# Top-k attention with a routed MLP: the comparison of row tile 7 written with an accumulator output

## The chip, the cores and the metric

The kernel runs on one core of a Trainium2 chip. The metric is the device time of one execution in microseconds (us), and the number that counts is the median of several runs.

The engines are named as in the profile: PE is TensorE's matmul, PEld its weight load, DVE is VectorE, ACT is ScalarE, POOL is GpSimd, SP is SyncE, which issues most of the DMA transfers.

## The reference

Attention of 8 batches, 8 heads, 576 tokens, head size 64. Only the 32 highest scores of each row take part in the softmax. The result then goes through a layer that skips some tokens and sends each of the others to one of 8 experts.

```python
scores = scale * np.matmul(q, k.transpose(0, 1, 3, 2))
kth = np.partition(scores, -top_k, axis=-1)[..., -top_k:-top_k + 1]
mask = scores >= kth
scores = np.where(mask, scores, -1000000000.0)
...
attn = attn / (np.sum(attn, axis=-1, keepdims=True) + 1e-09)
return np.matmul(attn, v).astype(np.float32)

skip_score = x @ w_skip
do_compute = skip_score > 0
...
e_idx = np.argmax(logits, axis=1)
...
    h = np.maximum(xc[mask] @ w1[e], 0.0)
    y[mask] = gate_w[mask, None] * (h @ w2[e])
out[do_compute] = xc + y
```

## The kernel before

**Tiling.** The 64 heads are taken in 32 pairs. The two heads of a pair have 2 x 576 rows of scores, which are cut into nine row tiles of 128 rows, numbered `i` = 0 to 8; the middle one holds 64 rows of each head. A row tile of pair `p` has the running number `s = 9 p + i`.

**What is done for a row tile** (`row`, line 651):
- PE computes the 128 x 576 scores into one of three PSUM row buffers `r` (`qk`, line 670).
- DVE finds the eight highest of each of seven chunks (`chunk`, line 679, tile `cand`) and from these the 24 highest of the row (`cand`, lines 685 and 687, tile `cl`).
- ACT copies the scores out of PSUM into an SBUF tile `xc` (`take`, line 698); `xc` has three buffers. With this the PSUM row buffer is free again.
- ACT marks what is above the 24th score and counts it (`above_out`, line 693, with an accumulator output, which the profile shows as an instruction of its own on ACT).
- POOL multiplies the marked scores (`push_out`, line 701) and writes seven fill values (`fill`, line 710), both into `xw`.
- DVE takes the eight highest of `xw` (`window`, line 720, tile `wn`); the eighth is the 32nd highest score.
- The penalty is then written: a 128 x 576 tile in bf16 that is not zero where the score is below the 32nd highest (`below_out`, line 712, tile `PEN`). For seven of the nine row tiles it is an activation on ACT (line 717). For the two in `BELOW = (3, 7)` (line 28) it is a `tensor_scalar` on DVE (line 715).

**What uses it.** Per pair, PE computes the scores again, transposed, and adds the penalties with matmuls of `PEN` against `nbi`, which hold -2^120 on the diagonal (`block`, line 811). ACT exponentiates (line 832, `PT` and `PR`), and PE multiplies with the values (lines 879 to 898). POOL also adds two of the exponentials (line 858) and splits the next pair's inputs into high and low parts (lines 580 and 583).

**What sets the order.** The instructions of the attention part are put in order before the build by a planner (`Plan`, line 181): each task has an engine, an assumed duration and a due time from hand-set tables, and every engine then runs its list in that order. The planner's duration for the penalty on DVE is 0.42 us (line 748), in both kernels. A wait that matters below is in line 741: `take` of row tile `s` may start only when the penalty of row tile `s - 3` has been written (`OUTB[-3:-2]`), since both use the same buffer of `xc`. So the penalty of row tile 7 holds back `take` of row tile 1 of the next pair.

After the attention part (up to about 870 us) follow the experts (lines 1037 to 1223), which the change does not touch.

Of the kernel before, what the change touches and what calls it, by code (L numbers as in the profile page):

```python
# [9 lines left out]
F32 = mybir.dt.float32  # L10
# [4 lines left out]
OP = mybir.AluOpType  # L15
# [12 lines left out]
BELOW = (3, 7)  # L28
# [12 lines left out]
def tile_kernel(ctx, tc, q, k, v, w_skip, w_gate, w1, w2, out):  # L41
    nc = tc.nc
# [4 lines left out]
    P = 128  # L47
# [15 lines left out]
    cp = ctx.enter_context(tc.tile_pool(name="cp", bufs=1))  # L63
# [587 lines left out]
    def row(s):  # L651
        p, i = divmod(s, NR)
        i2 = p % NQ
        PEN[p] = PEN_[p % 2]
        h = Hold(RW, 1)
# [56 lines left out]
        def below_out():  # L712
            pen, least = PEN[p][:, PS * i + REM:PS * (i + 1)], WN[p][:, i, 7:8]
            if i in BELOW:
                nc.vector.tensor_scalar(pen, XC[s], least, None, op0=OP.is_lt)
            else:
                nc.scalar.activation(pen, XC[s], AF.Relu, bias=least, scale=-1.0)  # L717

# [27 lines left out]
        OUTW.append(wx)  # L746
        WINS.setdefault(p, []).append(wx)
        kx = PENNED[s] = A(*(("DVE", 0.42) if i in BELOW else ("ACT", 0.672)), s + D_["rf"] + J("rf"), below_out, wx, TU.get(p - 2))
        OUTB.append(kx)
        if i == NR - 1:  # L750
            FLAGGED[p] = A("POOL", 0.47, s + 3, flags, kx, WINS[p])

    XC, XW, OUTB, OUTW, WINS, PUSHD = {}, {}, [], [], {}, {}
    PS = S + REM
    PEN_ = [(ap_ if j == (NP - 1) % 2 else sp_).tile([P, NR * PS + REM], BF, name=f"PEN{j}") for j in range(2)]
    for t in PEN_:
        nc.vector.memset(t[:, 0:NR * PS].rearrange("p (i c) -> p i c", c=PS)[:, :, 0:REM], 0.0)
        nc.vector.memset(t[:, NR * PS:], 0.0)

# [32 lines left out]
    def block(p, whats, rb, turned):  # L792
# [5 lines left out]
        for half in range(2):  # L798
# [6 lines left out]
            for y, (h, c0, m, o, kc) in enumerate(whats):  # L805
                for c, i, a, z in hv[y][half][2]:
                    penalties.append((half, rb[:, O + c:O + c + z - a], PEN[p][:, PS * i + REM + c0 - o:PS * i + REM + c0 - o + P], nbi[:, a:z]))
        todo = penalties + products if turned else products + penalties
# [753 lines left out]
```

## Time and profile before

| what | value |
|---|---|
| time, median of 3 runs | 1147.55 us (1146.78, 1147.55, 1151.96) |
| time of the profiled execution | 1154.68 us |
| its span, from the first to the last instruction | 1152.8 us |
| PE busy | 1102.5 us, 96% of the span |
| DVE busy | 985.7 us, 85% |
| ACT busy | 889.3 us, 77% |
| POOL busy | 806.6 us, 70% |
| mean granted TensorE clock | 0.979 of full speed |
| DVE line 715, both row tiles, 64 instructions | 64.2 us busy, 1002 ns mean |

The busy shares are means over the whole span. In the attention part PE and DVE are both busy for some 98% of a pair's time, so which of them sets the time is read from the idle stretches of single pairs and from what ended them. The times of single instructions come from the profiled execution, which took 7.1 us longer than the median of the runs.

### The profile page before, as it was taken

Reading aid. Unit: us, or ns where it says so; the run is one execution under the profiler, and the core shown is the slowest. Engines: PE = TensorE matmul, PEld = TensorE weight load, DVE = VectorE, ACT = ScalarE, POOL = GpSimd, SP = SyncE. Lnnn points to the kernel's source line nnn. Section 1 sums busy time; section 2 is a strip of 40 time slices with the busy share of each in tenths; the row PEclk is TensorE's granted clock in tenths of the full one; section 3 lists DMA queues with packets and bytes.
Section 4 is the critical chain, followed back from the end, with each engine's and each line's share of the span. In section 5 each row is a group of like instructions: output and inputs, shape, how many; then the busy total and the mean of one; then the engine's idle time right before and its main releaser. Section 6 shows DMA issues by size and latency. Waiting matters only on the chain.

```text
span 1152.8 us, 37624 instructions
## 1 busy us (share of the span) xinstructions
PE 1102.5 (96%) x12995; PEld 934.2 (81%) x12995; DVE 985.7 (85%) x5002; ACT 889.3 (77%) x1838; POOL 806.6 (70%) x1236
## 2 busy tenths in 40 slices
PE   7799999999899999999998999999999999999996
PEld 5678888888788888888787888888787888999995
DVE  7999999999999999999999999999986556755541
ACT  4889999999799999998998999999884534444420
POOL 5878888888688888988998988888895212222211
PEclk7899999999899999999999999999999999999998
DMA  5655555665555555665654465555238465555300
GB/s 114 145 133 116 136 125 124 139 138 135 122 115 117 132 130 115 141 147 112 145 116 105 106 141 135 121 122 111 64 90 282 149 206 164 173 176 165 120 19 26
DMA packets 239257, 149.08 MB, mean 129 GB/s; under 512 B 141656, under 2 KB 204632, under 8 KB 239056
## 3 DMA queue, kind: packets, MB, share of 16 engines
q1 hardware_dynamic: 232192, 136.19, 48.5%
q0 software_dynamic: 3840, 9.47, 2.4%
q8 instruction: 105, 1.72, 0.6%
q10 hardware_dynamic: 3024, 0.90, 0.3%
q14 instruction: 96, 0.79, 0.2%
HBM read 76.57 MB, written 25.31 MB: 88 GB/s over the span
## 4 chain that ended last, share of the span: by engine, by line
PE 65%; DVE 19%; ACT 5%; issue 4%; SPq 2%; POOL 2%; DMA 1%; ACTq 0%; POOLq 0%; DVEq 0%
PE r L811 14%; PE r L670 11%; PE pa L879 7%; DVE cand L679 7%; PE py L1168 4%; PE py L1170 4%; PE py L1169 4%; PE ph L1145 3%; PE ph L1146 3%; PE ph L1147 3%; DVE wn L720 3%; DVE cl L685 3%; DVE cand L687 2%; PE pa L896 2%; PE pa L882 2%
## 5 line engine op out<-in xcount | busy, mean ns | idle before, releaser
L679 DVE MAX8 cand<-r 128x8 f32<-128x82 f32 (+1 forms) x2016 | 391.3, 233 | 11.2 <-PE r L670 7.2
L701 POOL TENSOR_TENSOR xw<-xc,r 128x576 f32<-128x576 f32 x288 | 370.6, 1287 | 19.2 <-ACT r L693 18.8
L693 ACT ACTIVATE r<-xc,cl 128x576 bf16<-128x576 f32 x288 | 226.5, 787 | 22.3 <-DVE cl L685 17.6
L720 DVE MAX8 wn<-xw 128x8 f32<-128x583 f32 x288 | 215.8, 750 | 3.3 <-POOL xw L701 3.3
L698 ACT ACTIVATE xc<-r 128x576 f32<-128x576 f32 x288 | 188.9, 657 | 32.0 <-DVE cl L685 24.0
L811 PE MATMUL r<-QH,KK 128*128 128x320 f32 (+1 forms) x640 | 184.1, 315 | 1.2 <-ACT xc L698 0.5
L670 PE MATMUL r<-KK,QH 128*128 128x288 f32 x640 | 159.0, 338 | 22.8 <-ACT xc L698 15.4
L717 ACT ACTIVATE PEN<-xc,wn 128x576 bf16<-128x576 f32 x224 | 176.2, 789 | 2.8 <-DVE wn L720 2.5
L811 PE MATMUL r<-QL,KK 66*128 66x320 f32 (+1 forms) x640 | 174.0, 299 | 0.0
L832 ACT ACTIVATE PT<-r 128x576 f32<-128x576 f32 x256 | 164.1, 652 | 7.9 <-PE r L811 7.5
L685 DVE MAX8 cl<-cand 128x8 f32<-128x28 f32 (+2 forms) x864 | 162.2, 188 | 2.3
L1074 POOL DMA_INDIRECT out_dram<-ot,idx x24 | 24.4, 1015 | 189.2 <-DVE ot L1073 144.8
L670 PEld LDWEIGHTS r<-KK,QH 128*128 128x128 f32 x640 | 97.8, 193 | 61.4 <-ACT xc L698 24.3
L670 PE MATMUL r<-KK,QL 65*128 65x288 f32 x640 | 135.1, 302 | 1.5 <-DMA QL<-LO 1.3
L1037 ACT ACTIVATE hi<-raw 128x1024 fp32r<-128x1024 f32 x64 | 67.2, 1056 | 78.6 <-PE py L1170 70.6
L811 PE MATMUL r<-nbi,PEN 128*128 128x128 bf16 (+1 forms) x1632 | 127.4, 216 | 0.3
L1040 DVE TENSOR_TENSOR lo<-raw,hi 128x1024 fp32r<-128x1024 f32 x60 | 73.2, 1223 | 61.7 <-ACT hi L1037 61.3
L879 PE MATMUL pa<-PT,V 128*32 128x256 f32 (+1 forms) x2464 | 122.5, 330 | 0.7 <-ACT os L905 0.4
L811 PEld LDWEIGHTS r<-QH,KK 128*128 128x128 f32 x640 | 118.7, 191 | 3.5 <-ACT xc L698 2.0
L811 PEld LDWEIGHTS r<-QL,KK 66*128 66x128 f32 x640 | 119.8, 193 | 0.0
L710 POOL TENSOR_TENSOR xw<-wo,CN 128x7 f32<-128x7 f32 x288 | 64.7, 225 | 73.6 <-ACT r L693 68.4
L811 PEld LDWEIGHTS <-PEN 128*128 128x128 bf16 x1632 | 88.6, 99 | 21.5 <-issue 3.1
(277 smaller groups left out, 2548.1 us busy)
## 6 DMA issues: line engine op xcount, KB each, us to landing
raw<-in_moe_w_dram SPq DMA_DIRECT2D x64, 512.0 KB, 3.5
KK<-HI SPq DMA_DIRECT2D x62, 288.0 KB, 4.2
QH<-HI SPq DMA_DIRECT2D x124, 144.0 KB, 4.1
KK<-LO SPq DMA_DIRECT2D x62, 144.0 KB
QL<-LO SPq DMA_DIRECT2D x62, 144.0 KB, 2.7
raw<-in_k_dram SPq DMA_DIRECT2D x64, 128.0 KB, 2.6
V<-in_v_dram SPq DMA_DIRECT2D x32, 256.0 KB, 3.2
out_dram<-xd SPq DMA_DIRECT2D x28, 288.0 KB, 3.3
```

The costliest lines, as they stand in the source:

```text
L670: nc.tensor.matmul(R(u, w), t[0:k0, c:c + P], KH[i2][0:k0, HB * hd + u:HB * hd + w], start=(k0 == P and x == 0), stop=(k0 < P and x == len ...
L679: nc.vector.max(C[s][:, c], R(CH[c], CH[c + 1]))
L685: nc.vector.max(L[:, 4 * r:4 * r + 8], c)
L693: nc.scalar.activation(RR[s], XC[s], AF.Sign, bias=CL[p][:, i, 23:24], scale=-ODD / SMALL, accum_out=CN[:, s:s + 1])
L698: nc.scalar.activation(XC[s], R(), AF.Copy, scale=SMALL)
L701: nc.gpsimd.tensor_tensor(xw()[:, 0:S], XC[s], RR[s], op=OP.mult)
L717: nc.scalar.activation(pen, XC[s], AF.Relu, bias=least, scale=-1.0)
L720: nc.vector.max(WN[p][:, i], XW[s])
L811: nc.tensor.matmul(*ops, start=half not in [x[0] for x in todo[:j]], stop=half not in rest, skip_group_check=turned)
L832: return pl.add("ACT", 0.535, due + K["ex"] + FINE["ex"][at], lambda: nc.scalar.activation(dst, st["r"], AF.Exp, scale=scale), x, give=[h])
L879: nc.tensor.matmul(o, vt[:, a, kc, w:w + 32], pts[a][:, kc, qs:qs + n], start=(kc == 0), stop=False, tile_position=(0, 64 * u + w))
L1040: eng.tensor_tensor(WLO[w][i], WRAW[w][i], WHI[w][i], op=OP.subtract)
```

## The change

The penalty of row tile 7 gets a second scalar operation (add 0.0), which leaves its values as they are, and an accumulator output into a new tile `under` of one value per row, which nothing reads. The penalty of row tile 3 stays as it was. The planner sees the same tasks with the same durations, and every engine has the same instructions in the same order with the same waits, but for the form of these 32 instructions.

```diff
@@ -712,7 +712,10 @@
         def below_out():
             pen, least = PEN[p][:, PS * i + REM:PS * (i + 1)], WN[p][:, i, 7:8]
             if i in BELOW:
-                nc.vector.tensor_scalar(pen, XC[s], least, None, op0=OP.is_lt)
+                if i == BELOW[0]:
+                    nc.vector.tensor_scalar(pen, XC[s], least, None, op0=OP.is_lt)
+                else:
+                    nc.vector.tensor_scalar(pen, XC[s], least, 0.0, op0=OP.is_lt, op1=OP.add, accum_out=under)
             else:
                 nc.scalar.activation(pen, XC[s], AF.Relu, bias=least, scale=-1.0)
 
@@ -752,6 +755,7 @@
 
     XC, XW, OUTB, OUTW, WINS, PUSHD = {}, {}, [], [], {}, {}
     PS = S + REM
+    under = cp.tile([P, 1], F32, name="under")
```

## Rows read from the trace of the kernel before

**Rows 1.** Two pairs: length, busy us (count) of PE, PEld, DVE, ACT, POOL, PEclk, DMA.
```profile
225.63:251.07 25.44, 24.98 (x356) 20.97 (x356) 25.23 (x147) 24.12 (x54) 21.76 (x34) 1.00 0.58 130
...
302.27:332.70 30.43, 27.16 (x354) 23.00 (x353) 27.83 (x147) 24.34 (x54) 21.10 (x34) 0.89 0.48 109
```
**Rows 2.** PE around 227 us, by time: start, us, instruction, idle before it, its releaser.
```profile
226.80 0.61 PE L554 MATMUL pt<-identF,raw 128*128 128x128 f32 x4
227.87 0.53 PE L670 MATMUL r<-KK,QH 128*128 128x288 f32 x2 [0.46 <-ACT xc L698]
```
**Rows 3.** ACT in order of time, the same stretch.
```profile
225.78 0.37 ACT L905 ACTIVATE os<-pa 128x256 f32<-128x256 f32 x1
227.16 0.65 ACT L698 ACTIVATE xc<-r 128x576 f32<-128x576 f32 x1 [1.01 <-DVE cl L685]
```
**Rows 4.** DVE in order of time, the same stretch.
```profile
225.63 1.44 DVE L715 TENSOR_SCALAR PEN<-xc,wn 128x576 bf16<-128x576 f32 x1
226.99 0.18 DVE L685 MAX8 cl<-cand 128x8 f32<-128x28 f32 x1
```
**Rows 5.** Line 715: all its instructions, ns min/median/max, first and last start.
```profile
L715 DVE TENSOR_SCALAR PEN<-xc,wn x64: 497/952/3904, 35.3 to 857.1; 128x576 bf16<-128x576 f32 x64
```
**Rows 6.** Line 715 in 32 stretches, each around row tile 7's instruction: sum, mean.
```profile
sum 86.00, DVE 43.82; mean DVE 1.37
```
**Rows 7.** Line 715 in 32 stretches, each around row tile 3's instruction: sum, mean.
```profile
sum 67.00, DVE 20.34; mean DVE 0.64
```
**Rows 8.** POOL in order of time around 225.6 us.
```profile
225.40 1.29 POOL L701 TENSOR_TENSOR xw<-xc,r 128x576 f32<-128x576 f32 x1
226.64 0.49 POOL L710 TENSOR_TENSOR xw<-wo,CN 128x7 f32<-128x7 f32 x1
```
**Rows 9.** DVE in order of time around 240 us, row tile 3.
```profile
240.01 0.51 DVE L715 TENSOR_SCALAR PEN<-xc,wn 128x576 bf16<-128x576 f32 x1
240.43 0.19 DVE L685 MAX8 cl<-cand 128x8 f32<-128x28 f32 x1
```
**Rows 10.** POOL in order of time, the same stretch.
```profile
238.65 1.29 POOL L701 TENSOR_TENSOR xw<-xc,r 128x576 f32<-128x576 f32 x1
240.69 1.29 POOL L701 TENSOR_TENSOR xw<-xc,r 128x576 f32<-128x576 f32 x1 [0.75 <-ACT r L693]
```
**Rows 11.** Line 710: all its instructions, ns min/median/max.
```profile
L710 POOL TENSOR_TENSOR xw<-wo,CN x288: 191/201/507, 20.6 to 856.8; 128x7 f32<-128x7 f32 x144
```
**Rows 12.** Line 720: all its instructions, ns min/median/max.
```profile
L720 DVE MAX8 wn<-xw x288: 737/749/771, 25.6 to 858.4; 128x8 f32<-128x583 f32 x144
```
**Rows 13.** Groups by form on DVE: count, busy us, mean ns, idle before.
```profile
L687 DVE MATCH_VALUE_LOAD cand<-cl,cand 128x8 f32 x576 | 44.0, 76 | 3.6
...
L626 DVE TENSOR_TENSOR QL<-TT,QH 64x576 fp32r<-64x576 f32 x2 | 1.5, 744 | 0.0
```
**Rows 14.** Groups by form on ACT: the accumulator read of line 693.
```profile
L693 ACT ACTIVATION_READ_ACCUMULATOR r<-xc,cl 128x1 f32 x288 | 59.1, 205 | 0.0
```
**Rows 15.** Waits from 60 to 300 us: total us, times, longest.
```profile
ACT xc L698 <- DVE cl L685: 9.0, 9, 1.0
...
PE r L670 <- ACT xc L698: 4.1, 9, 0.5
```
**Rows 16.** Waits from 308 to 500 us.
```profile
PE r L670 <- ACT xc L698: 3.2, 7, 0.5
```
**Rows 17.** Waits from 690 to 860 us.
```profile
PE r L670 <- ACT xc L698: 1.8, 4, 0.5
```
**Rows 18.** DVE in order of time around 302.3 us.
```profile
302.27 3.90 DVE L715 TENSOR_SCALAR PEN<-xc,wn 128x576 bf16<-128x576 f32 x1
```
**Rows 19.** POOL in order of time, the same stretch.
```profile
303.09 1.27 POOL L701 TENSOR_TENSOR xw<-xc,r 128x576 f32<-128x576 f32 x1
304.33 1.53 POOL L583 TENSOR_TENSOR LO<-TT,HI 128x640 fp32r<-128x640 f32 x1
```
**Rows 20.** PE in order of time, the same stretch.
```profile
306.97 0.85 PE L670 MATMUL r<-KK,QH 128*128 128x288 f32 x2 [3.27 <-ACT xc L698]
```

## The prediction

> **What bounds the kernel now.** I first read the stretches of one pair, to see which engine has time left. A regular pair takes 25.44 us, of which PE is busy 24.98, DVE 25.23, ACT 24.12 and POOL 21.76 [rows 1]. PE and DVE are thus both nearly full, and neither can be called the bound by its share. So I looked next at where their idle time lies. PE's 0.46 us in that pair are one single gap: at 227.87 the next scores (line 670) start after an idle stretch of 0.46 us that ACT's copy of line 698 ended [rows 2]. That copy had itself waited 1.01 us and started at 227.16 [rows 3], which is 0.09 us after DVE's comparison of line 715 for row tile 7 ended (225.63 + 1.44 = 227.07) [rows 4]. The profile names another DVE line as the releaser, but the program says which it is: the copy of a row tile needs the `xc` buffer that the comparison three row tiles earlier reads. So once per pair the comparison of row tile 7 holds ACT, ACT holds PE, and the pair is longer by PE's gap.
>
> Why is that comparison so long? Over its 64 instructions line 715 lies between 497 and 3904 ns [rows 5], for one form and one shape. The 32 of row tile 7 sum to 43.82 us, 1.37 us each [rows 6], those of row tile 3 to 20.34 us, 0.64 us each [rows 7]. The difference is what POOL does at that moment. At row tile 7 POOL is in the product of line 701, from 225.40 to 226.69; the comparison starts at 225.63 and ends 0.38 us after that product [rows 4, 8]. At row tile 3 POOL is idle from 239.94 to 240.69, and the comparison, from 240.01 on, takes 0.51 us [rows 9, 10]. So the comparison stands still until POOL's instruction is over, and then takes the rest of its own time. The reverse is seen as well: POOL's tiny line 710 right behind it takes 0.49 us [rows 8], where 201 ns is its median [rows 11]. Other DVE work is not held: the 288 instructions of line 720, which read 583 elements from SBUF, lie between 737 and 771 ns throughout [rows 12].
>
> **The change part by part.** *What is removed.* 32 comparisons with their wait for POOL. In a regular pair one takes 1.44 us, and the next DVE instruction starts 226.99 - 225.63 = 1.36 us after it.
>
> *What is added.* 32 comparisons with accumulator output. The trace has no such instruction on DVE, so I bound it from rows. A DVE instruction with two inputs over 576 f32 elements takes 744 ns (line 626), and one with a single input over 583 takes 749 (line 720); this is the slower rate [rows 12, 13]; the unhindered comparison takes 497 [rows 5], so it runs at a faster rate, and the new form costs between 497 and 744 ns for its main part. I take 744, the side that speaks against the change. The accumulator has to be written out as well: on ACT that is an instruction of 205 ns [rows 14], and DVE's smallest one, the load of eight values in line 687, takes 76 [rows 13]. Both ends: 0.06 (as a start-to-start step) to 0.2 us; I take 0.1, nearer to DVE's own row. So the new one ends about 0.85 us after its start (0.55 to 0.95), if POOL doesn't hold it. The Trainium skill, "VectorE: DVE Perf Modes", section "Two Vector instructions with no wait between them", says that such an op is two instructions, the main one and an accumulator read; no run here shows it yet.
>
> *That it isn't held* is the step on which everything hangs. The trace speaks for it in one way: line 715, at the fast rate, is held by POOL, and line 720, one-input as well and at the slower rate, is never held in 288 times. The Trainium skill, "SBUF — State Buffer", section "Who interferes with whom", says that `tensor_scalar` in a two-port mode blocks against GpSimd for a whole instruction, and excepts the form that also writes out its accumulator; the first half agrees with the 1.44 us beside the 0.51 us, and for the exception no row of before can speak.
>
> *What it gives in a regular pair.* The comparison ends 1.44 - 0.85 = 0.59 us earlier (0.49 to 0.89). ACT is free for the copy from 226.15 on (225.78 + 0.37) [rows 3], so the copy moves by the same 0.59 us. PE is ready at 227.41 (226.80 + 0.61) [rows 2], and needs the copy 0.46 us earlier to have no gap. Up to an end of 0.98 us after its start the comparison closes PE's gap entirely, and all of the bounds lie below that. What is late next is PE itself, which has no other gap in such a pair. DVE must follow: it gets 1.36 - 0.77 = 0.59 us per pair back (0.77 is 0.85 less the 0.08 us by which one DVE instruction overlaps the next), more than the 0.46 by which PE gets faster. POOL has 3.7 us per pair to spare and is held less.
>
> *Sum.* The gaps of this kind: 4.1 us in 9 places, 3.2 us in 7 and 1.8 us in 4 [rows 15 to 17], together 9.1 us in 20 pairs. ACT's wait is 9.0 us in the first 9 of them [rows 15], 1 us each, so there is no shortage of waiting to take away. One pair stands by itself: at 302.27 the comparison took 3.90 us [rows 18], because two further POOL instructions got in before it, up to 305.86 [rows 19]; PE stood idle for 3.27 us [rows 20], the granted clock of this pair was 0.89, and it took 30.43 us in place of 25.44 [rows 1], 5.0 us more. Without the wait this goes: 5.0 us. In the other 11 pairs (the first, and those around the routing from 500 to 690 us and at the end) DVE's comparison gets shorter by 0.5 us or less, but I see no gap of PE that begins there; I count them at nothing (0 to 2 us of gain). In the profiled execution that is 1154.68 - 9.1 - 5.0 = 1140.6 us.
>
> The runs say how far that carries to the median. They are 1146.78, 1147.55 and 1151.96; the third is 4.4 us above the second, about what the one bad pair costs, and the profiled execution is higher still. I take it that the bad pair is an accident which the run at the median didn't have: 1147.55 - 9.1 = 1138.4, rounded to 1138 us, 0.8% faster. If every execution has it, the median becomes 1147.55 - 14.1 = 1133.4.
>
> **The rivals.** *The wait stays and the fast rate goes (slower).* If the accumulating form is held by POOL as the plain one is, it ends where POOL lets it and then needs 744 in place of 497 ns and the read: 0.25 + 0.06 to 0.2 = 0.3 to 0.45 us later. Each of the 20 gaps of PE grows by that, 6 to 9 us: 1153.5 to 1156.5, taken as 1155. It decides at one point: whether the wait is one of this operation or of its fast rate. Line 720 speaks for the rate, but it is another operation. The Trainium skill, "VectorE: DVE Perf Modes", section "The perf-mode tier table", gives `tensor_scalar` on f32 in SBUF twice the rate of a two-input operation, and counted alone it would speak against giving that rate up; the rows agree on the rate (497 beside 744 ns) but show that row tile 7 pays 1370.
>
> *Row tile 3 falls into POOL's product (slower).* It starts only 0.07 us after line 701 ends [rows 9, 10]. If the new rhythm brought DVE there earlier than POOL, it would be held as row tile 7 was: 1.36 - 0.42 = 0.94 us (0.42 is its present start-to-start step), which less the 0.59 won is 0.35 us of DVE per pair, 7 us in 20: 1154.5. Against it: between the two, DVE runs without a pause and POOL's work hangs on DVE's results, so they move together.
>
> *The form stays at the fast rate and is held as before (no change).* Then the change doesn't do what it says, and only the read is added: 0.06 to 0.2 us in 20 to 32 places, 1 to 6 us, around 1150.
>
> *PE is not really full (gain given back).* PE's ends are modelled, and behind the closed gap the next late result, an exponential or a chunk's maximum, may open another one. If half of the gain is lost: 1147.55 - 4.5 = 1143.
>
> **How the numbers follow.** About 0.5% (5.7 us) is what a measurement of this kernel can tell from no change. Forecast 0.72 (1133 to 1141, its middle 1138); half given back 0.10 (1143); fast rate and wait both kept 0.06 (1150); wait kept, rate lost 0.07 (1155); row tile 3 held 0.05 (1154.5). Faster by over 0.5%, below 1141.8: 0.74, the forecast and a little of the half. Slower, above 1153.3: 0.11, the two slow rivals without what little of them stays below. Same: 0.15. The range goes from 1132, a little below the case in which every run has the bad pair, to 1146, which takes in the half given back; above it and below it some 0.2 is left out.
>
> **What would show it.** In the profile of the changed kernel the instruction of row tile 7 should lie within a narrow band near 750 ns with a short second one behind it, none above 1 us; if it spreads as before, the wait has stayed. ACT's copy of line 698 should wait no more than 0.5 us for DVE, and the wait of line 670 for it, 9.1 us here, should be nearly gone. A regular pair should take about 24.98 us, with PE without a gap and DVE idle for some 0.3 us. POOL's line 710 behind row tile 7 should take 0.2 and not 0.49 us. Row tile 3 should stay at 0.64 us in the mean; above 1 us the second slow rival is at work. A pair of 25.4 us in spite of a short comparison would make the prediction wrong at PE, and a pair that is longer at DVE.

## The result, and the profile after

The changed kernel takes 1136.3 us (median of 6 runs, 1132.95 to 1140.07) against 1147.45 us before (6 runs, 1146.78 to 1155.0) on the same chips: a ratio of 0.9886, 95% interval 0.9853 to 0.9918. The forecast was 1138 us, with a range of 1132 to 1146. The profiled execution took 1134.66 us, 20.0 us less than that of before.

The page's summary of engines after the change (busy us, share of the span, instructions):

```profile
PE 1096.6 (97%) x12995; PEld 931.8 (82%) x12995; DVE 967.5 (85%) x5034; ACT 889.0 (78%) x1838; POOL 800.9 (71%) x1236
```

DVE has 32 instructions more and is busy 18.2 us less (985.7 before). The instructions of row tile 7 (line 718 now) and of row tile 3 (line 716) by operation, ns min/median/max:

```profile
L718 DVE TENSOR_SCALAR_CACHE_REDUCE PEN<-xc,wn x32: 787/794/817, 46.7 to 836.5; 128x576 bf16<-128x576 f32 x32
L718 DVE DVE_READ_ACCUMULATOR PEN<-xc,wn x32: 76/82/89, 47.4 to 837.3; 128x1 f32 x32
...
L716 DVE TENSOR_SCALAR PEN<-xc,wn x32: 494/502/1628, 35.2 to 824.9; 128x576 bf16<-128x576 f32 x32
```

Where line 715 spread from 497 to 3904 ns [rows 5], the new form stays within 30 ns, and it comes as two instructions. Row tile 3, which kept its form, sums to 20.52 us (20.34 in [rows 7]):

```profile
sum 96.00, DVE 20.52; mean DVE 0.64
```

One regular pair of the changed kernel, 186.35 to 211.15 us (length; busy us and count of PE, PEld, DVE, ACT, POOL; clock, DMA):

```profile
186.35:211.15 24.80, 24.80 (x363) 20.91 (x358) 24.59 (x148) 24.14 (x53) 21.55 (x33) 1.00 0.60 134
```

Against [rows 1] the pair is 0.64 us shorter. This is the shorter of two kinds: of the 19 pairs that took 25.2 to 25.65 us before, six now take 24.92 to 25.01 us and one 25.15, so the mean gain of the 19 is 0.56 us. PE has no gap left, and DVE is idle for 0.21 us, exactly as before. The places that answer to [rows 2 to 4] and [rows 8], in order of time on each engine (start, us, instruction, idle before):

```profile
222.20 0.79 DVE L718 TENSOR_SCALAR_CACHE_REDUCE PEN<-xc,wn 128x576 bf16<-128x576 f32 x1
222.92 0.08 DVE L718 DVE_READ_ACCUMULATOR PEN<-xc,wn 128x1 f32 x1
222.92 0.18 DVE L685 MAX8 cl<-cand 128x8 f32<-128x28 f32 x1
...
221.96 1.29 POOL L701 TENSOR_TENSOR xw<-xc,r 128x576 f32<-128x576 f32 x1
223.21 0.21 POOL L710 TENSOR_TENSOR xw<-wo,CN 128x7 f32<-128x7 f32 x1
...
223.09 0.65 ACT L698 ACTIVATE xc<-r 128x576 f32<-128x576 f32 x1 [0.38 <-DVE cl L685]
...
223.36 0.61 PE L554 MATMUL pt<-identF,raw 128*128 128x128 f32 x4
223.80 0.53 PE L670 MATMUL r<-KK,QH 128*128 128x288 f32 x2
```

The comparison starts 0.24 us after POOL's product (0.23 before) and now runs beside it: neither waits. POOL's line 710 takes 0.21 in place of 0.49 us. From the comparison's start to the next DVE work it is 222.92 - 222.20 = 0.72 us, where it was 1.36; the read adds nothing to see. ACT's copy waits 0.38 in place of 1.01 us.

### The profile page after: what moved, and what is told of

Its sections match the earlier page's. It is cut to its first block, busy times and chain, and to the rows that moved or that the text cites. A ratio compares the mean times of both kernels' runs of the same rounds, so it can differ in the third digit from the quotient of the medians.

```text
span 1132.9 us, 37656 instructions
## 1 busy us (share of the span) xinstructions
PE 1096.6 (97%) x12995; PEld 931.8 (82%) x12995; DVE 967.5 (85%) x5034; ACT 889.0 (78%) x1838; POOL 800.9 (71%) x1236
## 4 chain that ended last, share of the span: by engine, by line
PE 44%; DVE 41%; issue 6%; ACT 3%; POOL 2%; DMA 2%; SPq 1%; ACTq 0%; POOLq 0%; DVEq 0%
DVE cand L679 16%; PE r L815 8%; DVE wn L723 7%; PE r L670 6%; DVE cl L685 6%; DVE cand L687 5%; PE py L1172 4%; PE py L1174 4%; PE py L1173 4%; PE pa L883 3%; PE ph L1149 3%; PE ph L1151 3%; PE ph L1150 3%; PE pt L883 1%; DVE xb L939 1%
## 5 line engine op out<-in xcount | busy, mean ns | idle before, releaser
L710 POOL TENSOR_TENSOR xw<-wo,CN 128x7 f32<-128x7 f32 x288 | 59.3, 206 | 68.3 <-ACT r L693 65.8
```

## Experiments

The theory after the result: POOL held the plain form, the accumulating form isn't held, and what DVE's step gets shorter (1.36 to 0.72, 0.64 us) is what a pair gets shorter, since DVE sets the pair. The rivals: the second operation does it and not the accumulator; the way over ACT's copy to PE's gap is the cost, as my sum had it; PE, busy without a gap, is the bound now.

**The second operation without the accumulator.**

```diff
-                    nc.vector.tensor_scalar(pen, XC[s], least, 0.0, op0=OP.is_lt, op1=OP.add, accum_out=under)
+                    nc.vector.tensor_scalar(pen, XC[s], least, 0.0, op0=OP.is_lt, op1=OP.add)
```

> Row tile 7's comparison keeps the second scalar operation (add 0.0) and loses the accumulator output; all else as in the changed kernel. Theory (the accumulator output is what takes the instruction off the fast rate, and only so off POOL's hold): the second operation alone changes nothing, row tile 7 takes some 1.43 us as in the kernel before, a regular pair 25.43 us, the median 1147.5 us. Rival (any second operation takes the fast rate away): some 0.75 to 0.79 us in a narrow band, a regular pair of 24.7 to 24.8 us, 1135 to 1137 us.

Measured: 1150.9 us against 1151.28 before on the same chips, ratio 1.0007 (0.9983 to 1.0032). All of line 718, and one pair:

```profile
L718 DVE TENSOR_SCALAR PEN<-xc,wn x32: 568/1429/4252, 46.2 to 854.2; 128x576 bf16<-128x576 f32 x32
...
187.68:213.12 25.44, 24.93 (x364) 20.93 (x358) 25.23 (x147) 24.13 (x53) 21.77 (x33) 1.00 0.57 131
```

The median of 1429 ns (some 1.42 us for row tile 7 before) and the pair of 25.44 us are those of before. The add alone changes nothing; the accumulator output does it.

**Both row tiles with the accumulator.**

```diff
-                if i == BELOW[0]:
+                if i not in BELOW:
```

> Both row tiles, 3 and 7, have the accumulator output. Theory (DVE's start-to-start steps set a regular pair): row tile 3, which POOL doesn't hold in a regular pair, steps 0.72 in place of 0.42 us, so a regular pair takes 24.79 + 0.30 = 25.09 us; with about 20 such pairs, less some 1.7 us from the pairs in which row tile 3 was held, 1141 us. Rival (PE, which shows no gap in the changed kernel, sets the pair): DVE's 0.30 us goes into DVE's slack of 0.2 us per pair, a regular pair 24.8 to 24.9 us, 1135 to 1138 us.

Measured: 1139.63 us, ratio to before 0.9907 (0.989 to 0.9923). All of line 718, and one pair:

```profile
L718 DVE TENSOR_SCALAR_CACHE_REDUCE PEN<-xc,wn x64: 781/795/816, 35.1 to 840.4; 128x576 bf16<-128x576 f32 x64
...
186.36:211.47 25.11, 24.87 (x362) 20.93 (x358) 24.90 (x149) 24.12 (x53) 21.50 (x33) 1.00 0.58 133
```

Row tile 3 isn't held in such a pair, so for it the slower form is a loss of 0.30 us, and the pair is longer by 0.31 (25.11 against 24.80), within 0.01 us what DVE's step costs. DVE's idle 0.21 us did not take it up; it stands there still (25.11 less 24.90). The total came out at 1139.6 where 1141 was expected.

**The way over ACT taken out, in the kernel before.** Four buffers of `xc`, nothing else:

```diff
-            XC[s] = wk.tile([P, S], F32, name="xc", bufs=3)
+            XC[s] = wk.tile([P, S], F32, name="xc", bufs=4)
```

> The kernel before, with four buffers of xc in place of three, every engine's list in the same order: ACT's copy no longer needs the buffer that row tile 7's comparison reads. Theory (DVE's step of 1.36 us is the cost): PE's gap behind the copy goes or moves, but a regular pair stays at 25.43 us, 1147.5 us. Rival (the cost is the way over ACT's copy to PE's gap, as the prediction's sum had it): the gap of 0.46 us closes, a regular pair takes 24.8 to 24.98 us, 1136 to 1139 us.

Measured: 1152.18 us against 1151.28, ratio 1.0019 (0.9999 to 1.0038). One pair, around its row tile 7 DVE, ACT and PE in order of time, and a wait from 60 to 500 us (total us, times, longest):

```profile
187.45:212.93 25.48, 25.01 (x362) 20.96 (x358) 25.27 (x148) 24.32 (x53) 21.77 (x33) 1.00 0.57 131
...
198.54 1.44 DVE L715 TENSOR_SCALAR PEN<-xc,wn 128x576 bf16<-128x576 f32 x1
199.90 0.18 DVE L685 MAX8 cl<-cand 128x8 f32<-128x28 f32 x1
...
198.96 0.65 ACT L698 ACTIVATE xc<-r 128x576 f32<-128x576 f32 x1
...
199.68 0.61 PE L554 MATMUL pt<-identF,raw 128*128 128x128 f32 x4
200.04 0.51 PE L670 MATMUL r<-KK,QH 128*128 128x288 f32 x2
...
PE r L811 <- ACT PT L832: 6.7, 17, 0.4
```

ACT's copy starts 1.02 us before the comparison ends, and PE has no gap behind line 554. So the copy's wait came from the shared buffer; the entry in line 741, which is unchanged here, only puts the lists in order. The comparison is as long as before, and so is the pair. This shows that the chain comparison, copy, PE's gap was there but was not what the pair cost: with the chain gone, PE waits in other places (line 811 for an exponential, 0.4 us in 17 pairs).

**Less work on PE, in the changed kernel.** The row sums leave out the last key tile, so the probabilities differ, and with them the routing and the experts' time; only the attention part can be compared.

```diff
-                                nc.tensor.matmul(o, ones, pt, start=first, stop=(kc > NM - 2 and z), tile_position=(0, r0))
-                            else:
-                                nc.tensor.matmul(o, oneh[:, a], pr[:, cs], start=first, stop=True, tile_position=(0, r0))
+                                nc.tensor.matmul(o, ones, pt, start=first, stop=(kc == NM - 1 or (kc == NM - 2 and z)), tile_position=(0, r0))
```

> The changed kernel with less work on PE: the row sums leave out the last key tile (the matmuls of one-hot columns against PR, two groups of 0.22 us and one of 0.05 us start to start per pair, some 0.5 us). Theory (DVE sets a regular pair in the changed kernel): 24.79 us per pair as before, 1135 to 1136.5 us. Rival (PE is full at 24.79 us, as its busy time without a gap says): a regular pair of some 24.3 us, 1136.3 - 25 x 0.5 = 1124 us.

Measured: 1260.35 us, of which the part behind the attention has grown by some 125 us (from row tile 3's comparison of the last pair to the end it is 433 us in place of 308). One pair of the attention part:

```profile
183.19:208.00 24.81, 24.60 (x344) 20.50 (x338) 24.60 (x149) 24.12 (x53) 21.48 (x33) 1.00 0.58 134
```

Twenty matmuls fewer, and the pair stays at 24.8 us. PE's busy time falls by 0.2 us and it has idle time again; so its 24.80 us without a gap was not a full PE. From the first of row tile 3's comparisons to the last, the attention part is 3.4 us shorter than in the changed kernel's profile, where the rival expected some 12; 4.0 us of gain lie in the first two pairs and the last, 1.1 us of loss in the pair near 610 us, and the 19 regular pairs differ by 0.1 us in all.

DVE's idle time is 0.21 us once more, and what ends it says which engine sets the pair. In the pair of [rows 1], in the changed kernel's pairs of 24.80 us and in those of this run it is six stretches of 34 or 35 ns, each between two instructions of DVE itself; none ends with another engine. Two of them in the kernel before, in order of time on DVE (235.78 to 235.81 and 236.00 to 236.04):

```profile
235.40 0.38 DVE L679 MAX8 cand<-r 128x8 f32<-128x82 f32 x2
235.81 0.19 DVE L685 MAX8 cl<-cand 128x8 f32<-128x28 f32 x1
236.04 0.09 DVE L687 MATCH_VALUE_LOAD cand<-cl,cand 128x8 f32 x1
```

DVE sets the pair, before the change and after it.

**A slower form with two inputs.** Does POOL hold only the fast rate, or also a slower form that reads a second tensor?

```diff
-                    nc.vector.tensor_scalar(pen, XC[s], least, 0.0, op0=OP.is_lt, op1=OP.add, accum_out=under)
+                    nc.vector.tensor_tensor(pen, XC[s], least.to_broadcast([P, S]), op=OP.is_lt)
```

> Row tile 7's comparison as a two-input operation on DVE: the scores against the 32nd highest, read as a second tensor with step 0; no accumulator output. Theory A (what POOL holds is the fast rate, and only that): the operation runs at the slower rate, 744 ns as line 626, unheld; a step of 0.66 us, a regular pair of 25.43 - 1.36 + 0.66 = 24.73 us. Theory B (what POOL holds is any second read of a DVE instruction, which the fast rate needs too): it waits for POOL's product and then needs 0.25 us more than the plain form, 1.6 to 1.7 us, a regular pair of 25.65 to 25.7 us, and a time some 5 us above that of before.

Measured: 1160.79 us against 1152.33, ratio 1.0069 (1.0039 to 1.0099). All of line 718, one pair, and the place in it on DVE and POOL:

```profile
L718 DVE TENSOR_TENSOR PEN<-xc,wn x32: 853/1696/1757, 46.1 to 863.1; 128x576 bf16<-128x576 f32 x32
...
190.61:216.29 25.68, 24.95 (x364) 20.97 (x358) 25.47 (x147) 24.12 (x53) 22.02 (x33) 1.00 0.57 129
...
201.67 1.69 DVE L718 TENSOR_TENSOR PEN<-xc,wn 128x576 bf16<-128x576 f32 x1
...
201.45 1.29 POOL L701 TENSOR_TENSOR xw<-xc,r 128x576 f32<-128x576 f32 x1
202.69 0.72 POOL L710 TENSOR_TENSOR xw<-wo,CN 128x7 f32<-128x7 f32 x1
```

Theory A is out, and what theory B expected of the operation and of the pair came: the operation waits for POOL's product (to 202.74) and then needs 0.62 us, 0.24 us more than the plain form, and POOL's line 710 behind it waits longer, 0.72 us. The time is 8.5 us above that of before, where some 5 were expected; the regular pairs account for 5 to 6 of them, and the rest stays open. So the hold is not one of the fast rate alone. That the fast form is held for the same reason, a second stream read from SBUF which the accumulating form and line 720 lack, fits all the forms but is not shown: no run sees how many streams a form reads, and only the two-input form has its second one by its edit. The Trainium skill, "SBUF — State Buffer", section "Who interferes with whom", says that an operation with two SBUF inputs contends with a GpSimd instruction that reads SBUF; this run agrees (1.69 us beside POOL's product).

**A mixture, beside the changed kernel once more.** The accumulator output on row tile 3 as well, but only in eight pairs in which POOL held it:

```diff
-                if i == BELOW[0]:
+                if i == BELOW[0] and p not in (0, 17, 18, 19, 21, 24, 29, 30):
```

> The changed kernel once more, beside the next one on the same chip. Theory: a regular pair of 24.79 us, the comparison of row tile 7 within 0.78 to 0.82 us, 0.986 to 0.99 of the time before.

> The changed kernel with the accumulator output on row tile 3 as well in eight pairs (0, 17, 18, 19, 21, 24, 29, 30), those in which POOL held row tile 3 for a step above 0.72 us in the changed kernel's profile. Theory (each pair goes by DVE's steps): the steps over 0.72 us sum to 1.8 us, so 1.5 to 3 us faster than the changed kernel, with its regular pairs at 24.79 us. Rival (in these pairs DVE has idle time, and what it saves is waited away): no difference.

Measured: the changed kernel 1134.48 us (ratio to before 0.9847, 0.9811 to 0.9883), the mixture 1133.65 us (0.9839, 0.9812 to 0.9865). The changed kernel's ratio lies a little below the 0.986 to 0.99 expected; its comparison (0.79 to 0.81 us) and its pair (24.80 us) came as expected. The mixture is the faster one, as expected, but by 0.8 us and not 1.5 to 3, and that is smaller than either interval; whether the mixture is better stays open. Its regular pair is 24.80 us.

**Three more profiles of the kernel before.** Each profile so far in which row tile 7 is held had one comparison or more above 2.4 us. Nothing is changed here:

> The kernel before once more, for one profile: how often does a comparison of line 715 lose its place to two POOL instructions, and what does it cost? Theory (the bad pair is an accident of single executions): comparisons above 1.7 us in some of the profiles and at other pairs, each of them making its pair 3 to 5.5 us longer; a profile without any is at 1147 to 1149 us. Rival (the bad pair has its place in the program): the same pair at 302 us again, in each profile.

> As the look before it: the kernel before, for a second profile. Theory: other pairs or none are bad; rival: the pair at 302 us again.

> As the two looks before it: the kernel before, for a third profile. Theory: other pairs or none are bad; rival: the pair at 302 us again.

Measured: 1156.16, 1154.86 and 1152.61 us. A comparison of row tile 7 above 3.9 us stands in pair 4 of the first (148.5 us) and pair 25 of the second (694 us); the third has none of row tile 7. In the first, DVE and POOL in order of time:

```profile
148.47 4.26 DVE L715 TENSOR_SCALAR PEN<-xc,wn 128x576 bf16<-128x576 f32 x1
152.66 0.18 DVE L685 MAX8 cl<-cand 128x8 f32<-128x28 f32 x1
...
148.25 1.28 POOL L701 TENSOR_TENSOR xw<-xc,r 128x576 f32<-128x576 f32 x1
149.50 0.19 POOL L710 TENSOR_TENSOR xw<-wo,CN 128x7 f32<-128x7 f32 x1
149.66 1.26 POOL L701 TENSOR_TENSOR xw<-xc,r 128x576 f32<-128x576 f32 x1
150.89 1.52 POOL L583 TENSOR_TENSOR LO<-TT,HI 128x640 fp32r<-128x640 f32 x1
```

It is the picture of [rows 18, 19]: POOL's line 710 gets in before the waiting comparison, unhindered at 0.19 us, and POOL's next two follow. These two pairs took 29.79 and 29.57 us in place of 25.44. So the bad pair of row tile 7 is an accident of single executions and has no fixed place. That a profile without one would stand at 1147 to 1149 us was wrong: the third has 1152.61, with a comparison of row tile 3 of 2.51 us in pair 24 and the last pair longer than usual. That comparison does have a place: in pair 24 row tile 3 took 2.49 to 2.51 us in five of the seven profiles in which row tile 7 is held (the first and third here, and those of the second operation alone, of four buffers and of two inputs), and 1.25 or 1.26 us in the other two and in the three in which only row tile 7 has the accumulator. The long case makes its pair some 1.3 us longer (27.10 beside 25.84).

## Why the prediction was right, and where it was off

- **POOL no longer holds row tile 7: right.** 32 of 32 within 787 to 817 ns. The bound of 744 from line 626 was 50 ns short, the read of 0.1 us was 0.08, and the end at 0.80 us (222.92 + 0.08 - 222.20) lies by the 0.85 that I took. The step is 0.72, where I had 0.77.
- **What a regular pair gains: the mechanism of this term was wrong and its size too small.** I took the gain as PE's gap, 0.46 us, and DVE's 0.59 us as enough to follow. It is the other way round. Four `xc` buffers closed the gap and gave nothing; 0.30 us more on DVE cost 0.31 us; less work on PE took nothing off a regular pair. Such a pair gains at most DVE's step, 0.64 us, and came out at 24.80 and not 24.98; the mean gain over 19 pairs is 0.56 us, since seven of them came out longer, at 24.92 to 25.15, for a reason that no run looked for. I had looked at where PE's idle time lies and not at DVE's, which in the same pair never ends with another engine. The sentence that failed is "What is late next is PE itself": PE's busy time must have counted waiting that isn't a gap, as the run with less work on PE shows. The row misled me in its size as well: behind line 554 the next scores came 227.87 - 226.80 = 1.07 us later before and 0.44 after, so PE stood at least 0.63 us and not 0.46; the modelled end of line 554, 0.61 us after its start, hid the rest.
- **The sum.** By pairs (from one start of row tile 3's comparison to the next) the two profiles differ by 20.0 us: 10.6 in 19 pairs that took 25.2 to 25.65 us before (I had 9.1 in 20), 5.8 in the bad pair (I had 5.0), and 3.6 in all the rest, which I counted at nothing with 2 as the end. Of these 2.5 lie in one pair near 610 us, which also varies by over 3 us between the later profiles of the kernel before, so I don't put them down to the change. That the forecast of 1138 us came near is in part luck: the sum took PE's gap for the gain, and this gap of 0.46 us happened to lie near the 0.56 us that the pairs gained.
- **The bad pair as an accident: right.** It stood in four of seven profiles of kernels whose row tile 7 is held, at pairs 4, 10, 13 and 25, and in none of the five whose row tile 7 has the accumulator (no comparison of either row tile above 1.64 us there). How often it comes was not measured apart from that, and the runs of before spread for other reasons too: on the chips of the later experiments its median was 1151.3 and 1152.3 us, and the ratio of the changed kernel accordingly 0.9847. The median of the first six, 1147.45, went down by 11.2 us, a little more than the 9.1 of my sum, whose two errors (too little per pair, no gain elsewhere) point the same way.
- **The rivals.** Wait kept, rate lost: its price was about right (8.5 us above before, where I had 7.5), but it belongs to the two-input form, and by another sum: a regular pair got 0.24 us longer there (25.68 beside 25.44), where I had 0.3 to 0.45 per gap of PE. Fast rate and wait kept: it is what the second operation alone does, without a price (ratio 1.0007). Row tile 3 falling into POOL's product did not happen in regular pairs (502 ns median, 0.64 us mean as before). Half given back: the regular pairs gave back nothing of the 0.46 us.

## What to carry to other kernels

Where the same short instruction on one engine takes 0.5 us here and 1.4 us there, look at what the neighbouring engine does at these moments before anything else; a nominally slower form that doesn't meet the neighbour can be the faster one. It is worth it only where the meeting happens: on row tile 3, which met nobody, the same form cost 0.30 us per pair. And of two engines that both look full, a change of a known size on one of them (0.3 us more here, some 0.5 us less there) tells which sets the time. The busy share did not. What ended the idle time of each would have: PE's 0.46 us ended with ACT, which had waited for DVE, and DVE's 0.21 us never ended with another engine.

## What the runs showed of the hardware that was not expected

- A comparison of 576 elements with an accumulator output takes 795 ns and its read 82 ns, yet the next DVE work starts 720 ns after it: the read costs nothing that can be seen.
- A waiting DVE instruction can lose its place several times in a row to POOL: behind the product that it had met, POOL's line 710, its next product and line 583 went first, and it stood for 3.9 to 4.3 us; one such accident made a pair 4.1 to 5.4 us longer (29.57 and 30.79 us beside 25.43). In [rows 1] the granted clock of such a pair fell to 0.89; PE had stood still for 3.27 us in it.
- A PE that shows 24.80 us busy in 24.80 us had room: with 20 matmuls fewer per pair a regular pair took 24.81 us.
